# Batch 0 in two token ranges, ordered first loads, and a table of convolution blocks and priorities per batch, in a pooled-attention and gated-FFN kernel

## The chip, the cores and the metric

One core of a Trainium2 chip. The metric is the time of one execution on the device, in microseconds (us), median of several runs. The span in a profile is the time from the first to the last instruction of the profiled run and is about 2 us shorter. Engines are called PE (matmul), DVE (vector), ACT (scalar), POOL (GpSimd) and SP (which issues the stores and a few loads), as the profile does. The granted clock is the share of PE's full clock that the profile records.

## The reference, cut to what matters

```python
# q, k, v: (8 batches, 8 heads, 576 tokens, 64)
k_p = k.reshape(B, H, 72, 8, D).mean(axis=3)          # pool 8 tokens into one
v_p = v.reshape(B, H, 72, 8, D).mean(axis=3)
attn = softmax(q @ k_p^T / sqrt(D)) @ v_p             # -> x: (8, 576, 512)
h = np.maximum(x @ w_in, 0.0)                         # w_in: 512 x 1024
conv_out = sum_k conv_w[k] * hp[:, k:k + S, :]        # 3 taps along the tokens, per channel
gate = 1.0 / (1.0 + np.exp(-conv_out))
out = (h * gate) @ w_out                              # w_out: 1024 x 512
```

Inputs and output are fp32. The kernel computes in bf16, and takes the sigmoid as (1 + tanh)/2, so that one set of activation functions serves exp and tanh.

## The kernel before

The program is built by a small planner. Each piece of work is an `Op` with an assumed duration on each engine that may do it, its dependences, and a priority. The planner walks forward in assumed time, gives each engine the ready piece with the lowest priority number, and writes the instructions out in that order. Each engine's list is then fixed. A piece that may run on DVE or ACT is placed when the plan is made, not on the chip.

```python
class Planner:
    N_PS = 4            # PSUM slots, each 2 x 512 fp32
    WARM = 24.0         # fill PE's idle time with matmuls on zeros up to here
    ...
        for e, c in per.items():
            t0 = min(c)[0]
            c = [x for x in c if x[0] <= t0 + 0.02]
            s, p, i = min(c, key=lambda x: (x[1], x[2]))      # p is the priority
```

The 1024 hidden channels are eight blocks of 128. The three-tap convolution of a block exists in two forms. On PE it is three matmuls with diagonal weights for each half of the tokens. Off PE it is three scalings on DVE or ACT, two additions on DVE, and a tanh on ACT:

```python
    def conv_off(b, f, pr):
        ...
        for kk in (1, 0, 2):
            pl.add(f"cp{kk}.{b}.{f}", {"DVE": 0.225, "ACT": 0.59}, ...)   # cv = factor * shifted hT
        for kk in (0, 2):
            pl.add(f"ca{kk}.{b}.{f}", "DVE", 0.375, ...)                  # cv[1] += cv[kk]
        pl.add(f"tanh.{b}.{f}", "ACT", 0.59, ...)
    def conv_pe(b, f, pr):
        ...
        for kk in range(3):
            for i in range(2):
                nc.tensor.matmul(out=t[:, i, 0:HC], lhsT=dw[:, f, kk, :], rhs=hT[m][:, f, ...], ...)
        pl.add(f"conv.{b}.{f}", "PE", 0.745, ...)
    def conv(b, f, pr):
        conv_off(b, f, pr) if f in OFF[b] else conv_pe(b, f, pr)
        # then on DVE for every block: tg = tg + 1, and gT = tg * hT   (the gate product)
```

`OFF` is (1, 3, 5, 7) for every batch. Priorities follow one rule for all batches: `mm1` (the product with `w_in`) of block f at 8b + f, its convolution 1.3 later, the next batch's attention at fixed offsets, `mm2` (the product with `w_out`) of a pair of batches at 11.0, 14.5, 10.5, 12.5 and 15.5. Batch 0's k is loaded as fp32 on SP's queue, q and v as bf16 on POOL's queue.

The softmax here doesn't subtract the row's maximum and nothing guards it: scores larger than these inputs give would overflow.

Of the kernel before, what the change touches and what calls it, by code (L numbers as in the profile page):

```python
# [14 lines left out]

class Op:
# [3 lines left out]
class Planner:  # L20
# [7 lines left out]
    WARM = 24.0  # L28
# [37 lines left out]
    def order(self):  # L66
# [10 lines left out]
        live = set()  # L77
# [4 lines left out]
        while avail:  # L82
            best = None
            per = {}
            for i, t in avail.items():
                o = ops[i]
                st = t
                if o.take is not None and o.take not in held:
                    if not slots:
                        continue  # L90
                    st = max(st, min(slots.values()))
                cand = None
                for e, d in o.eng.items():
                    s = max(st, free.get(e, 0.0))
                    if cand is None or s + d < cand[0]:
                        cand = (s + d, s, e)
                _, s, e = cand
                per.setdefault(e, []).append((s, o.prio, i))
# [14 lines left out]
            if e == "PE" and s < self.WARM and s - free.get(e, 0.0) > 0.3:  # L113
                f0 = max(free.get(e, 0.0), 0.6)
                x = min(slots, key=lambda y: (slots[y], y)) if slots else None
                if x is not None and slots[x] <= f0 and s - f0 > 0.3:
                    self.gaps[i] = (s - f0, x)
# [7 lines left out]
            if o.give is not None:  # L125
                slots[held[o.give]] = o.done
            out.append((s, e, d, o))
# [12 lines left out]
def kernel(  # L140
# [40 lines left out]
    k_f = st("k_f", [KR, KT, 512], FP32)  # L181
# [21 lines left out]
    OFF = [(1, 3, 5, 7) for b in range(B)]  # L203
# [13 lines left out]
    def warm(gap, x):  # L217
        t = pp.tile([P, 2, 512], FP32, name="psw", tag=f"ps{x}")
        for _ in range(min(int((gap - 0.2) / 0.1), 60)):
            nc.tensor.matmul(out=t[:, 0, 0:P], lhsT=zero[:, 0:P], rhs=zero[:, 0:P], start=True, stop=True)  # L220
# [30 lines left out]
    def load_k(b, prio):  # L251
        m = b % 2
        if b == 0:
            for i in range(2):
                def fn(e, i=i):
                    nc.sync.dma_start(out=k_f[:, 3 * i:3 * i + 3, :], in_=rows_k(0)[:, 3 * i:3 * i + 3, :])
                pl.add(f"ldk0.{i}", "SP", 0.6, fn, writes=[("kf", i)], prio=prio, nbytes=H * S * D * 2)
        else:
            def fn(e):
                nc.gpsimd.dma_start(out=k_b[m], in_=rows_k(b))  # L260
            pl.add(f"ldk{b}", "POOL", 0.9, fn, writes=[("k", m)], prio=prio, nbytes=H * S * D * 4)

    def load_v(b, prio):
        m = b % 2

        def fn(e):
            nc.gpsimd.dma_start(out=v_b[m], in_=rows_v(b))
        pl.add(f"ldv{b}", "POOL", 0.9, fn, writes=[("v", m)], prio=prio, nbytes=H * S * D * 4)
# [15 lines left out]
    def consts():  # L284
# [6 lines left out]
        pl.add("ident", "POOL", 0.6, fn, writes=["ident"], prio=-50)  # L291
# [17 lines left out]
        def fn(e):  # L309
            t = slot("cw")  # L310
            nc.tensor.transpose(out=t[:, 0, 0:24], in_=cw_raw, identity=identf)
        pl.add("cwT", "PE", 0.1, fn, reads=["cwr", "identf"], writes=["cwp"], prio=-46, take="cw")

        def fn(e):
            nc.vector.tensor_scalar(out=cw, in0=slot("cw")[:, 0, 0:24], scalar1=2.0, scalar2=None, op0=OP.mult)
        pl.add("cw", "DVE", 0.1, fn, reads=["cwp"], writes=["cw"], prio=-45, give="cw")

        for f in range(n_fb):
            for kk in range(3):
                def fn(e, f=f, kk=kk):  # L320
                    s = cw[:, kk * n_fb + f:kk * n_fb + f + 1]
                    if e == "ACT":
                        nc.scalar.activation(out=dw[:, f, kk, :], in_=ident, func=ACT.Copy, scale=s)
                    else:
                        nc.vector.tensor_scalar(out=dw[:, f, kk, :], in0=ident, scalar1=s, scalar2=None, op0=OP.mult)
                pl.add(f"dw{f}.{kk}", {"ACT": 0.3, "DVE": 0.2}, 0, fn, reads=["cw", "ident"],
                       writes=[("dw", f, kk)], prio=-3 + 0.5 * f)
# [13 lines left out]
    def attn_k(b, pr):  # L341
        m = b % 2
        if b == 0:
            for i in range(2):
                def fn(e, i=i):
                    c = slice(3 * i, 3 * i + 3)
                    nc.vector.tensor_tensor(out=kp1[:, c, :], in0=k_f[:, c, 0:256], in1=k_f[:, c, 256:512], op=OP.add)
                pl.add(f"kp1.{b}.{i}", "DVE", 0.875, fn, reads=[("kf", i)], writes=[("kp1", i)], prio=pr)
# [34 lines left out]
    def attn_v(b, pr):  # L383
        m = b % 2

        def fn(e):
            nc.vector.tensor_tensor(out=vp1, in0=v_b[m][:, :, 0:256], in1=v_b[m][:, :, 256:512], op=OP.add)
        pl.add(f"vp1.{b}", "DVE", 1.14, fn, reads=[("v", m)], writes=["vp1"], prio=pr)

        def fn(e):  # L390
            nc.vector.tensor_tensor(out=vp2, in0=vp1[:, :, 0:128], in1=vp1[:, :, 128:256], op=OP.add)
        pl.add(f"vp2.{b}", "DVE", 0.61, fn, reads=["vp1"], writes=["vp2"], prio=pr)
# [3 lines left out]
        pl.add(f"va.{b}", "DVE", 0.34, fn, reads=["vp2", ("v8", m)], writes=[("va", m)], prio=pr)  # L396
# [20 lines left out]
    def attn_s(b, h, pr):  # L417
        m = b % 2
        key = ("sc", b, h)

        def fn(e):
            t = slot(key)
            for par in range(2):
                nc.tensor.matmul(  # L424
                    out=t[0:Sp, par, 0:HC],
                    lhsT=kTz[m][:, par, h * Sp:(h + 1) * Sp],
                    rhs=qT[m][:, :, h * A:(h + 1) * A],
                    start=True, stop=True,
                )
        pl.add(f"sc.{b}.{h}", "PE", 0.25, fn,  # L430
               reads=[("kTz", m, 0), ("kTz", m, 1), ("qT", m, 0), ("qT", m, 1), ("qT", m, 2)],
               writes=[("scp", b, h)], prio=pr, take=key)

        def fn(e):
            nc.scalar.activation(  # L435
                out=attnT[m][:, h, :].rearrange("p (c i x) -> p i c x", i=2, x=32),
                in_=slot(key)[0:Sp, :, 0:HC].rearrange("p i (c x) -> p i c x", x=32),
                func=ACT.Exp, scale=1.0 / 64.0,
            )
        pl.add(f"exp.{b}.{h}", "ACT", 0.55, fn, reads=[("scp", b, h)], writes=[("at", m, h)], prio=pr, give=key)  # L440

    def attn_av(b, t, pr):
# [11 lines left out]
        pl.add(f"av.{b}.{t}", "PE", 0.36, fn, reads=[("at", m, h) for h in range(H)] + [("va", m)],  # L454
# [36 lines left out]

    def mm1(b, f, pr):
        m = b % 2
# [14 lines left out]
        pl.add(f"relu.{b}.{f}", "ACT", 0.55, fn, reads=[("hp", b, f)], writes=[("hT", m, f)], prio=pr, give=key)  # L508
# [3 lines left out]
    def conv_off(b, f, pr):  # L512
# [4 lines left out]
        for kk in (1, 0, 2):  # L517
# [7 lines left out]
            pl.add(f"cp{kk}.{b}.{f}", {"DVE": 0.225, "ACT": 0.59}, 0, fn, reads=[("hT", m, f), ("hz", m), "cw"],  # L525
# [10 lines left out]
    def conv(b, f, pr):  # L536
# [14 lines left out]
        pl.add(f"g.{b}.{f}", "DVE", 0.375, fn, reads=[("tg", i3), ("hT", m, f)], writes=[("gT", (b // 2) % 2, f, b % 2)],  # L551
               prio=pr)

    def conv_pe(b, f, pr):
# [11 lines left out]
        pl.add(f"conv.{b}.{f}", "PE", 0.745, fn, reads=[("hT", m, f), ("hz", m)] + [("dw", f, kk) for kk in range(3)],  # L566
# [9 lines left out]
    def mm2(pair, tiles, pr):  # L576
# [4 lines left out]
        for x, t in enumerate(tiles):  # L581
            halves = [0] if t < 4 else ([0, 1] if t == 4 else [1])

            def fn(e, x=x, t=t):
                a = slot(key)
                for c in range(n_fb):
                    nc.tensor.matmul(out=a[:, x, :], lhsT=g[:, c, t * P:(t + 1) * P], rhs=w_out[:, c, :],  # L587
                                     start=(c == 0), stop=(c == n_fb - 1))
            pl.add(f"mm2.{pair}.{t}", "PE", 1.74, fn,
                   reads=[("gT", pair % 2, c, y) for c in range(n_fb) for y in halves] + [("wo", 0), ("wo", 1)],  # L590
                   writes=[("op", pair, t)], prio=pr, take=key)
# [12 lines left out]
    def loads(b, prio):  # L604
        load_k(b, prio)
        load_q(b, 1 if b else 3, prio + 0.01)
        load_v(b, prio + 0.02)

    def attn(b):
        o = 8.0 * (b - 1)  # L610
        attn_k(b, o - 2.0)
        attn_q(b, [o - 1.5, o - 1.3, o - 1.1])
        attn_v(b, o + 0.0)
        for h in range(H):
            attn_s(b, h, o + 0.55 * h)
        for t in range(n_t):
            attn_av(b, t, o + 5.0 + 0.4 * t)
# [4 lines left out]
    loads(1, -20)  # L622
    weights_out(-25)
    attn(0)
    for b in range(B):
# [5 lines left out]
        for f in range(n_fb):  # L631
            mm1(b, f, o + f)
            conv(b, f, o + f + 1.3)
        p = b // 2
        if b % 2 == 0:
            mm2(p, (0, 1), o + 11.0)
            mm2(p, (2, 3), o + 14.5)
        else:
            mm2(p, (4,), o + 10.5)
            mm2(p, (5, 6), o + 12.5)  # L640
            mm2(p, (7, 8), o + 15.5)
# [37 lines left out]
```

## Time and profile before

The time is 246.21 us (244.66 to 247.72, 3 runs); the profiled span is 243.0 us.

| stage | what sets the pace | number |
|---|---|---|
| start, to the first `xT,w_in` matmul | loads, then one chain through DVE, ACT, PE | 25.42 us |
| middle | PE | 97% of 82 to 182 us |
| end, after the last gate product | `mm2` of four tiles, copy, store | 12.3 us (243.0 - 230.7) |

The page of the kernel before: busy time of each engine with its share of the span, then two rows of forty equal slices (tenths of busy PE, tenths of granted PE clock), then the chain of work that ended last.

```profile
PE 217.2 (89%) x1877; PEld 153.1 (63%) x1877; DVE 174.1 (72%) x470; ACT 165.5 (68%) x269; POOL 26.5 (11%) x47
...
PE   8566996589979999899999999999999999999691
...
PEclk9996799959999999999999999999999999999999
...
PE 56%; DVE 19%; ACT 19%; DMA 3%; issue 1%; ACTq 0%; DVEq 0%; POOLq 0%
```

PE leads the chain. Its weak slices stand in the first quarter and at the end. The timeline of the kernel before shows the start (columns: start, duration, engine, line, operation, output<-input, and in brackets the idle time before it):

```profile
8.50 0.51 PE L407 MATMUL psb<-ident,q_b 128*128 128x128 bf16 x6 [2.30 <-DMA q_b<-in_q_dram]
...
9.52 0.94 DVE L347 TENSOR_TENSOR kp<-k_f 96x768 bf16<-96x768 f32 x1
...
14.70 4.41 ACT L435 ACTIVATE attnT<-psf 72x576 bf16<-72x576 f32 x8
...
25.42 1.84 PE L500 MATMUL psf<-xT,w_in 128*128 128x288 bf16 x7
```

The second half of k is pooled only at 9.52 us, the exps over all tokens start at 14.70, and then all five token tiles of the attention output must pass before `xT,w_in` starts.

Busy time by stretch, kernel before (columns: from:to and length in us; busy us and instruction count of PE, weight loads, DVE, ACT, POOL; granted clock; DMA share; GB/s):

```profile
36.00:42.00 6.00, 4.26 (x45) 3.27 (x44) 5.92 (x15) 5.48 (x10) 0.58 (x1) 1.00 1.27 194
42.00:48.00 6.00, 3.38 (x45) 2.23 (x45) 5.86 (x15) 4.27 (x8) 1.56 (x2) 0.97 1.15 202
48.00:54.00 6.00, 4.80 (x48) 4.17 (x46) 5.03 (x14) 2.61 (x4) 0.36 (x1) 0.50 1.04 146
...
82.00:134.00 52.00, 50.64 (x452) 35.88 (x450) 44.00 (x115) 40.55 (x67) 2.63 (x3) 1.00 0.48 104
134.00:182.00 48.00, 46.51 (x414) 32.44 (x413) 32.92 (x96) 36.02 (x59) 0.00 (x0) 1.00 0.15 48
```

From 36 to 48 us DVE is full and PE is not; after that the clock is halved for six microseconds. From 82 us on PE is full and DVE has room: 76.9 busy of 100 us.

The end, in the chain of the kernel before (start, duration, what):

```profile
230.25 0.47 DVE gT L550
230.72 0.05 issue
230.77 7.31 PE psf L587 x33
...
238.15 1.01 ACT osb L595
```

### The profile page before, as it was taken

Reading aid. Unit: us, or ns where it says so; the run is one execution under the profiler, and the core shown is the slowest. Engines: PE = TensorE matmul, PEld = TensorE weight load, DVE = VectorE, ACT = ScalarE, POOL = GpSimd, SP = SyncE. Lnnn points to the kernel's source line nnn. Section 1 sums busy time; section 2 is a strip of 40 time slices with the busy share of each in tenths; the row PEclk is TensorE's granted clock in tenths of the full one; section 3 lists DMA queues with packets and bytes.
Section 4 is the critical chain, followed back from the end, with each engine's and each line's share of the span. In section 5 each row is a group of like instructions: output and inputs, shape, how many; then the busy total and the mean of one; then the engine's idle time right before and its main releaser. Section 6 shows DMA issues by size and latency. Waiting matters only on the chain.

```text
span 243.0 us, 4692 instructions
## 1 busy us (share of the span) xinstructions
PE 217.2 (89%) x1877; PEld 153.1 (63%) x1877; DVE 174.1 (72%) x470; ACT 165.5 (68%) x269; POOL 26.5 (11%) x47
## 2 busy tenths in 40 slices
PE   8566996589979999899999999999999999999691
PEld 8444775467656766666768667676767767656340
DVE  2597399989699997995499657933987659447500
ACT  2192399649795996769857967687949957657421
POOL 7843010212111220000000000000000000000000
PEclk9996799959999999999999999999999999999999
DMA  7999999999994998052204412020202101102214
GB/s 171 203 199 208 207 210 194 199 126 147 172 191 96 182 184 186 29 101 86 86 3 108 79 46 86 3 86 3 86 0 89 43 26 63 72 21 83 86 62 153
DMA packets 20617, 26.59 MB, mean 109 GB/s; under 512 B 2396, under 2 KB 14516, under 8 KB 20596
## 3 DMA queue, kind: packets, MB, share of 16 engines
q0 software_dynamic: 15024, 15.67, 40.4%
q1 hardware_dynamic: 5572, 10.63, 12.6%
q8 instruction: 14, 0.23, 0.4%
q14 instruction: 7, 0.06, 0.1%
HBM read 32.52 MB, written 9.44 MB: 173 GB/s over the span
## 4 chain that ended last, share of the span: by engine, by line
PE 56%; DVE 19%; ACT 19%; DMA 3%; issue 1%; ACTq 0%; DVEq 0%; POOLq 0%
PE psf L587 25%; PE psf L500 17%; ACT hT L506 5%; PE psf L563 4%; ACT attnT L435 4%; PE psf L424 4%; DVE xx L465 3%; DMA q_b<-in_q_dram 3%; PE psb L479 3%; ACT osb L595 3%; DVE cv L524 2%; DVE cv L529 2%; PE psb L407 2%; ACT cv L522 2%; ACT tg L533 2%; ACT tg L570 2%
## 5 line engine op out<-in xcount | busy, mean ns | idle before, releaser
L500 PE MATMUL psf<-xT,w_in 128*128 128x288 bf16 x512 | 72.3, 288 | 0.7
L587 PE MATMUL psf<-w_out,gT 128*128 128x512 bf16 x288 | 65.9, 379 | 2.4 <-DVE gT L550 1.9
L500 PEld LDWEIGHTS <-w_in 128*128 128x128 bf16 x512 | 50.0, 98 | 15.4 <-issue 2.0
L506 ACT ACTIVATE hT<-psf 128x576 bf16<-128x576 f32 x64 | 41.5, 651 | 13.4 <-PE psf L500 13.2
L587 PEld LDWEIGHTS <-gT 128*128 128x128 bf16 x288 | 27.7, 98 | 32.5 <-DVE gT L550 2.6
L524 DVE TENSOR_SCALAR cv<-hT,cw 128x576 bf16<-128x576 bf16 x76 | 24.2, 367 | 28.4 <-ACT hT L506 28.2
L435 ACT ACTIVATE attnT<-psf 72x576 bf16<-72x576 f32 x64 | 39.9, 652 | 0.6 <-PE psf L424 0.5
L595 ACT COPY osb<-psf 128x1024 f32<-128x1024 f32 (+1 forms) x20 | 18.5, 927 | 25.2 <-PE psf L587 25.2
L533 ACT ACTIVATE tg<-cv 128x576 bf16<-128x576 bf16 x32 | 21.8, 687 | 11.8 <-DVE cv L529 11.7
L550 DVE TENSOR_TENSOR gT<-tg,hT 128x576 bf16<-128x576 bf16 x64 | 29.1, 455 | 0.8
L563 PE MATMUL psf<-hT,dw 128*128 128x288 bf16 x192 | 29.0, 286 | 0.0
L529 DVE TENSOR_TENSOR cv<-cv 128x576 bf16<-128x576 bf16 x64 | 28.5, 445 | 0.4
L424 PE MATMUL psf<-qT,kTz 128*72 128x288 bf16 x128 | 24.8, 287 | 3.6 <-DVE qT L413 1.9
L545 DVE TENSOR_SCALAR tg<-tg 128x576 bf16<-128x576 bf16 x64 | 19.5, 304 | 11.7 <-ACT tg L533 11.7
L465 DVE TENSOR_TENSOR xx<-psf,rr 128x512 bf16<-128x512 f32 x40 | 27.1, 684 | 0.2
L479 PE MATMUL psb<-perm,xx 128*128 128x128 bf16 x160 | 17.6, 240 | 5.3 <-DVE xx L465 4.7
L570 ACT ACTIVATE tg<-psf 128x576 bf16<-128x576 f32 x32 | 20.7, 646 | 0.8
L563 PEld LDWEIGHTS <-dw 128*128 128x128 bf16 x192 | 18.2, 97 | 4.5
L424 PEld LDWEIGHTS <-kTz 128*72 128x72 bf16 x128 | 14.4, 114 | 8.3 <-issue 4.7
L452 PE MATMUL psf<-vaug,attnT 72*128 72x65 bf16 x320 | 16.3, 196 | 2.8 <-ACT attnT L435 1.3
L479 PEld LDWEIGHTS <-xx 128*128 128x128 bf16 x160 | 11.9, 106 | 10.3 <-DVE xx L465 8.0
L452 PEld LDWEIGHTS <-attnT 72*128 72x128 bf16 x320 | 14.3, 100 | 5.4 <-ACT attnT L435 3.3
(46 smaller groups left out, 181.0 us busy)
## 6 DMA issues: line engine op xcount, KB each, us to landing
out_dram<-osb SPq DMA_DIRECT2D x16, 512.0 KB, 2.8
v_b<-in_v_dram POOLq DMA_DIRECT2D x8, 576.0 KB, 11.0
k_b<-in_k_dram POOLq DMA_DIRECT2D x7, 576.0 KB, 11.4
q_b<-in_q_dram POOLq DMA_DIRECT2D x7, 576.0 KB, 10.3
k_f<-in_k_dram SPq DMA_DIRECT2D x2, 576.0 KB, 5.8
w_in<-in_moe_w_in_dram POOLq DMA_DIRECT2D x4, 256.0 KB, 10.9
w_out<-in_moe_w_out_dram POOLq DMA_DIRECT2D x2, 512.0 KB, 14.6
out_dram<-osb SPq DMA_DIRECT2D x4, 256.0 KB, 2.0
```

Source lines behind the costliest of these rows:

```text
L424: nc.tensor.matmul(out=t[0:Sp, par, 0:HC], lhsT=kTz[m][:, par, h * Sp:(h + 1) * Sp], rhs=qT[m][:, :, h * A:(h + 1) * A], start=True, stop= ...
L435: nc.scalar.activation(out=attnT[m][:, h, :].rearrange("p (c i x) -> p i c x", i=2, x=32), in_=slot(key)[0:Sp, :, 0:HC].rearrange("p i (c ...
L452: nc.tensor.matmul(out=a[:, h // 4, c:c + D + 1], lhsT=attnT[m][:, h, u0:u0 + 128], rhs=vaug[m][:, h, :], start=True, stop=True)
L465: nc.vector.tensor_tensor(out=xx[i3].rearrange("p (g h e) -> p g h e", g=2, h=4), in0=av_view()[:, :, :, 0:D], in1=rr[i3].rearrange("p (g ...
L479: nc.tensor.transpose(out=a[:, 0, c * P:(c + 1) * P], in_=xx[i3][:, c * P:(c + 1) * P], identity=perm)
L500: nc.tensor.matmul(out=t[:, i, 0:HC], lhsT=w_in[:, c, f * P:(f + 1) * P], rhs=xT[m][:, c, i * HC:(i + 1) * HC], start=(c == 0), stop=(c == ...
L506: nc.scalar.activation(out=hT[m][:, f, 2:S + 2].rearrange("p (i x) -> p i x", i=2), in_=slot(key)[:, :, 0:HC], func=ACT.Relu, scale=0.5)
L524: nc.vector.tensor_scalar(out=cv[y][:, kk, :], in0=src, scalar1=s, scalar2=None, op0=OP.mult)
L529: nc.vector.tensor_tensor(out=cv[y][:, 1, :], in0=cv[y][:, 1, :], in1=cv[y][:, kk, :], op=OP.add)
L550: nc.vector.tensor_tensor(out=gT[(b // 2) % 2][:, f, o:o + S], in0=tg[i3], in1=hT[m][:, f, 2:S + 2], op=OP.mult)
L563: nc.tensor.matmul(out=t[:, i, 0:HC], lhsT=dw[:, f, kk, :], rhs=hT[m][:, f, 1 + kk + i * HC:1 + kk + (i + 1) * HC], start=(kk == 0), stop= ...
L587: nc.tensor.matmul(out=a[:, x, :], lhsT=g[:, c, t * P:(t + 1) * P], rhs=w_out[:, c, :], start=(c == 0), stop=(c == n_fb - 1))
```

## The change

The intent: start `mm1` of batch 0 when two thirds of its tokens are ready; load in the order of need on one queue; take more convolution blocks off PE, by a table for each batch, and set every group of priorities by a table, so that PE, DVE and ACT are filled together; shorten the end. The diff, cut to its core:

```diff
+PARAMS = {
+    "off": [(2, 3, 4, 7), (1, 3, 4, 5, 6), (0, 1, 2, 3, 5, 7), (0, 1, 2, 3, 4, 6, 7), (1, 2, 3, 4, 5, 6, 7), (0, 1, 2,
+        3, 4, 5, 6, 7), (0, 1, 2, 3, 4, 5, 6, 7), (0, 1, 2, 3, 4, 5, 6)],
+    "k": [-6.89, -4.22, ...], "q": [...], "v": [...], "s": [...], "ds": [...], "av": [...],
+    "conv": [4.85, 4.34, 4.9, 2.85, 2.38, 2.01, 3.44, 4.85],
+    "mm2": [6.99, 13.56, 11.95, 11.64, 14.87, ...],
+}
-    WARM = 24.0
+    WARM = 60.0
+    QUOTA = {"sc": 2, "o": 2}                  # at most two PSUM slots for scores, two for mm2
-    OFF = [(1, 3, 5, 7) for b in range(B)]
+    OFF = PARAMS["off"]
...
-                    nc.sync.dma_start(out=k_f[:, 3 * i:3 * i + 3, :], in_=rows_k(0)[...])
+                    nc.gpsimd.dma_start(out=k_b[0][:, 3 * i:3 * i + 3, :], in_=rows_k(0)[...])
...                                             # v of batch 0 in two halves; diagonal weights on POOL
+        parts = [(0, 6, (0, 1)), (6, 9, (2,))] if b == 0 else [(0, 9, (0, 1, 2))]     # scores and exps
...
+    def mm1_parts(b, f, pr):                   # batch 0: mm1 and relu in two token ranges
+        for x, (j0, j1, ts) in enumerate([(0, 24, (0, 1, 2)), (24, 36, (3, 4))]):
...
-            mm2(p, (4,), o + 10.5)
-            mm2(p, (5, 6), o + 12.5)
-            mm2(p, (7, 8), o + 15.5)
+            mm2(p, (4,), o + m2[2], 6 if last else n_fb)       # last pair: 6 of 8 channel blocks first
+            mm2(p, (5, 6), o + m2[3], 6 if last else n_fb)
+            for g in ((7,), (8,)) if last else ((7, 8),):
+                mm2(p, g, o + m2[4])
```

The table holds 52 blocks instead of 32, so 12 blocks stay on PE instead of 32.

## The prediction

"Unbroken" in this and the later texts is the time of an instruction from its start to the start of the next, when the next follows at once: an addition of a constant on DVE lasts 0.30 us by itself, and 0.22 us unbroken. Sums of such times are the work of an engine without waits.

> **What bounds the kernel now.** Page: PE 217.2 us busy of 243.0 (89%), DVE 174.1, ACT 165.5; chain 56% PE, 19% DVE, 19% ACT. Three stages:
>
> 1. Start. The first first-layer matmul (`xT,w_in`) runs at 25.42 us (timeline). Until then the chain is: DMA of `q_b` to 8.45, DVE on k to 11.64, eight exps on ACT 14.70 to 19.12 (waiting for all of q and k), then five attention tiles in a row.
> 2. Steady state. The chain's pattern recurs every 51.9 us per two batches, 26.0 per batch, with PE 96 to 99% busy per 20 us stretch (stages table), DVE 60 to 91%. PE-bound. Batches 0 and 1 are worse: between 36 and 54 us PE is idle 5.6 of 18 us behind DVE (98% busy from 36 to 48), and the granted clock falls to 0.50 at 48 to 54.
> 3. Tail. The last gate product ends at 230.72, then 33 second-layer matmuls take 7.31 us, the copy 1.01, the store about 3; PE waited some 3 us before.
>
> **What the change moves**.
> PE: convolution 192 to 72 matmuls; six take 0.74 us, so 20 blocks save 14.8. PE's unbroken work is about 201 us before (fillers excluded), 186 after.
> DVE: 40 more adds (0.37), 27 more scalings (0.22), some copies; 19 identity scalings leave for POOL. Unbroken about 163 before, 185 after; busy 174 to about 200.
> ACT: scalings 20 to 53 (0.67), some copies to DVE: 165 to about 183 busy.
> So DVE becomes a co-limit. The Trainium skill, "VectorE: DVE Perf Modes" (section on why `tensor_tensor` can't do 4×), caps adds at half the scalings' best rate; the trace agrees: 0.37 against 0.22 us for 576 columns.
>
> Start: k first at about 330 GB/s of fp32 source (estimate: bytes landed by 15 us), whole near 7 us, q near 10.5, v near 14; exps from about 10.5; three tiles, not five, gate the first matmul: about 20 us instead of 25.4.
> Tail: only 22 matmuls (4.8 us) follow the last gate product, the last store is half as large, and 18 matmuls fill PE's wait: 3 to 6 us less.
> Middle: per batch PE needs on average 23.3 us, DVE 23.0 unbroken. With both nearly full I expect waits: 24.5 per batch instead of 26.0.
>
> **Sum.** PE: 20 before the first matmul, 181 of remaining work, 3.8 after: 205. DVE: 20 + 176 + 9: 205 too. Before, the same PE sum is 226 against 243: 17 lost to waits and clock. After, I give 13: span 218, time about 221 us. Start's 5.5 and the tail's gain are all critical; of the conv's 14.8 about 10 should survive.
>
> **What would show it.** First `xT,w_in` matmul at 19 to 21.5 us; PE and DVE each near 200 busy, ACT 183; DVE's share of the chain 30% or more; 48 to 50 us per two batches; no half clock between 48 and 60 us (the Trainium skill, "TensorE: Matmul & The Clock Gate", Part 1: idle stretches halve the clock; the trace agrees at 0.50); under 9 us after the last gate product.
>
> **What would make it wrong.** The plan fixes each engine's order from assumed durations; where the chip differs (ACT scaling 0.67 against 0.59 assumed), two nearly full in-order engines stall each other, and only start and tail remain (about 235). Ordered loads could come late. The 21 POOL scalings may be slow and delay loads behind them. Tuned priorities could hide more: 212.

## The result, and the profile after

The changed kernel takes 220.31 us median (218.99 to 220.89, 4 runs), against 245.44 for the kernel before in the runs beside it. The ratio is 0.8957 (95% interval 0.8878 to 0.9036). Ratios here and below are the mean time of one kernel's fast runs over that of the other's in the same rounds, so they are not quite the ratio of the medians quoted. Executions over 1.5% slower than the fastest of the same kernel are left out of the means.

The page of the changed kernel, the same rows as above, with DVE's slices added:

```profile
PE 201.8 (93%) x1800; PEld 140.8 (65%) x1816; DVE 191.4 (88%) x531; ACT 175.0 (81%) x303; POOL 34.9 (16%) x71
...
PE   8987998799999999889989999999999999999992
...
DVE  0668299999999999999999999999999999999910
...
PEclk9996799999999999999999999999999999999998
...
DVE 58%; PE 21%; ACT 13%; DMA 3%; issue 2%; POOL 1%; another core or an unknown queue 1%; ACTq 0%; DVEq 0%; POOLq 0%
```

The chain has changed hands: DVE 58%, PE 21%. A reduced clock remains in the fourth and fifth slices, while the one near 50 us is gone. The start in the timeline of the changed kernel:

```profile
6.81 0.56 DVE L368 TENSOR_TENSOR kp<-k_b 96x768 bf16<-96x768 bf16 x1
...
9.35 0.51 PE L433 MATMUL psb<-ident,q_b 128*128 128x128 bf16 x6
...
12.08 4.87 ACT L464 ACTIVATE attnT<-psf 72x384 bf16<-72x384 f32 x16 [0.61 <-PE psf L453]
...
20.68 1.44 PE L531 MATMUL psf<-xT,w_in 128*128 128x384 bf16 x4 [0.52 <-DVE xT L515]
```

k is pooled 2.7 us earlier, q comes 0.85 us later (it now stands behind k on the one queue), and the first `xT,w_in` matmul runs at 20.68 instead of 25.42 us. But its first four matmuls take 1.44 us. The stretches of the changed kernel show why, and show the middle:

```profile
18.00:24.00 6.00, 5.06 (x36) 3.32 (x35) 3.92 (x9) 1.22 (x3) 5.94 (x19) 0.51 1.20 210
...
82.00:134.00 52.00, 49.03 (x459) 35.09 (x463) 51.36 (x138) 45.79 (x78) 3.49 (x5) 1.00 0.51 109
134.00:182.00 48.00, 46.70 (x425) 32.43 (x427) 47.75 (x145) 46.96 (x77) 0.00 (x0) 1.00 0.14 50
```

The clock is at 0.51 from 18 to 24 us, just where the first `mm1` runs. In the 100 us of the middle DVE is busy 99.1, PE 95.7 and ACT 92.8: three engines nearly full at once. The end, in the timeline of the changed kernel:

```profile
204.37 8.85 PE L642 MATMUL psf<-w_out,gT 128*128 128x512 bf16 x39
...
206.54 0.83 DVE L604 TENSOR_TENSOR gT<-tg,hT 128x576 bf16<-128x576 bf16 x2
...
207.43 5.51 PEld L642 LDWEIGHTS <-gT 128*128 128x128 bf16 x27 [0.27 <-DVE gT L604]
...
213.51 0.59 ACT L652 COPY osb<-psf 128x512 f32<-128x512 f32 x1 [1.18 <-remote]
```

After the last gate product (207.4) 9.8 us are left, 2.5 less than before. From the first `xT,w_in` to the end of the last `mm2` it is 192.5 us (20.7 to 213.2) instead of 212.7 (25.4 to 238.1), so 24.1 us a batch instead of 26.6. The shortening is not even. The 64 gate products (eight for each batch) can be counted in the two traces, as the `gT<-tg,hT` instructions of DVE in order of time: of the 25.8 us by which the span falls, 8.4 are gained by the end of the 16th (84.9 to 76.5 us), 5.8 from there to the 48th (102.9 to 97.1), 9.1 in the last sixteen (42.9 to 33.8), and 2.5 after the last.

### The profile page after: what moved, and what is told of

It is laid out like the page before. It is cut to its first block, busy times and chain, and to the rows that moved or that the text cites. A ratio compares the mean times of both kernels' runs of the same rounds, so it can differ in the third digit from the quotient of the medians.

```text
span 217.2 us, 4675 instructions
## 1 busy us (share of the span) xinstructions
PE 201.8 (93%) x1800; PEld 140.8 (65%) x1816; DVE 191.4 (88%) x531; ACT 175.0 (81%) x303; POOL 34.9 (16%) x71
## 4 chain that ended last, share of the span: by engine, by line
DVE 58%; PE 21%; ACT 13%; DMA 3%; issue 2%; POOL 1%; another core or an unknown queue 1%; ACTq 0%; DVEq 0%; POOLq 0%
DVE cv L583 12%; DVE cv L578 10%; PE psf L642 9%; DVE xx L495 8%; DVE gT L604 7%; PE psf L554 6%; ACT attnT L464 5%; DVE tg L599 5%; DMA q_b<-in_q_dram 3%; DVE vp L411 3%; DVE qT L439 2%; ACT cv L576 2%; DVE kp L372 2%; DVE kTz L400 2%; PE psf L531 2%
## 5 line engine op out<-in xcount | busy, mean ns | idle before, releaser
L554 PE MATMUL psf<-xT,w_in 128*128 128x288 bf16 x448 | 62.1, 286 | 1.2 <-DVE xT L515 0.5
L554 PEld LDWEIGHTS <-w_in 128*128 128x128 bf16 x448 | 42.9, 98 | 13.1 <-DVE xT L515 1.0
L583 DVE TENSOR_TENSOR cv<-cv 128x576 bf16<-128x576 bf16 x104 | 46.0, 449 | 0.4 <-DVE cv L578 0.2
L464 ACT ACTIVATE attnT<-psf 72x576 bf16<-72x576 f32 (+2 forms) x72 | 39.3, 613 | 1.1 <-PE psf L453 1.1
L576 ACT ACTIVATE cv<-hT,cw 128x576 bf16<-128x576 bf16 x53 | 39.2, 772 | 0.4 <-DVE cv L583 0.2
L587 ACT ACTIVATE tg<-cv 128x576 bf16<-128x576 bf16 x52 | 35.7, 695 | 3.0 <-DVE cv L583 2.4
L578 DVE TENSOR_SCALAR cv<-hT,cw 128x576 bf16<-128x576 bf16 x103 | 34.9, 363 | 2.6 <-ACT hT L538 2.5
L453 PE MATMUL psf<-qT,kTz 128*72 128x288 bf16 (+2 forms) x144 | 24.3, 271 | 2.2 <-DVE qT L439 0.6
L509 PEld LDWEIGHTS <-xx 128*128 128x128 bf16 x160 | 11.2, 102 | 9.2 <-DVE xx L495 5.8
L515 DVE COPY xT<-psb 128x512 bf16<-128x512 bf16 (+1 forms) x29 | 11.0, 390 | 2.4 <-PE psb L509 2.3
L287 POOL DMA_DIRECT2D v_b<-in_v_dram x9 | 7.5, 834 | 27.7 <-DVE vp L411 14.1
```

The source lines that it names most:

```text
L453: nc.tensor.matmul(out=t[0:Sp, par, 0:n], lhsT=kTz[m][:, par, h * Sp:(h + 1) * Sp], rhs=qT[m][:, 2 * c0:2 * c1, h * A:(h + 1) * A], start= ...
L464: nc.scalar.activation(out=attnT[m][:, h, :].rearrange("p (c i x) -> p i c x", i=2, x=32)[:, :, c0:c1, :], in_=slot(key)[0:Sp, :, 0:n].rea ...
L554: nc.tensor.matmul(out=t[:, i, 0:HC], lhsT=w_in[:, c, f * P:(f + 1) * P], rhs=xT[m][:, c, i * HC:(i + 1) * HC], start=(c == 0), stop=(c == ...
L576: nc.scalar.activation(out=cv[y][:, kk, :], in_=src, func=ACT.Copy, scale=s)
L578: nc.vector.tensor_scalar(out=cv[y][:, kk, :], in0=src, scalar1=s, scalar2=None, op0=OP.mult)
L583: nc.vector.tensor_tensor(out=cv[y][:, 1, :], in0=cv[y][:, 1, :], in1=cv[y][:, kk, :], op=OP.add)
```

## The experiments

My theory, T: the middle was bound by PE, the change takes 14.8 us off PE and fills DVE instead, and the priorities are needed to keep both full. Rival R1: the priorities alone do it. Rival R2: the table alone does it. Times are medians; "before" beside these runs was 245.64 to 246.54 us. The 95% intervals of the ratios reach 0.003 to 0.009 to each side.

| run | time, us | ratio to before |
|---|---|---|
| changed kernel | 220.31 | 0.8957 |
| a_off4: four blocks a batch again | 234.28 | 0.9504 |
| a_oldprio: old priorities again (3 fast runs of 4) | 234.74 | 0.9520 |
| a_base: both undone | 237.58 | 0.9665 |
| b_off: before, with the table alone | 241.28 | 0.9786 |
| a_dve, a_pe: changed, more DVE / PE work | 232.58, 227.83 | 0.9414, 0.9259 |
| b_dve, b_pe: before, more DVE / PE work | 250.18, 260.39 | 1.0183, 1.0587 |
| a_late: first loads later | 222.35 | 0.9059 |
| a_heat: batch 0's scores twice | 217.14 | 0.8844 |
| r_plan: a_heat, refitted | 215.83 | 0.8749 |
| r_pool: r_plan's way, one step to POOL | 251.26 | 1.0170 |

### Table and priorities, alone and together

```diff
 # a_off4                                        # a_oldprio
-    OFF = PARAMS["off"]                         -    "conv": [4.85, 4.34, 4.9, ...]
+    OFF = [(1, 3, 5, 7) for b in range(B)]      +    "conv": [1.3] * 8    (and all others as before)
 # a_base: both.   # b_off: the kernel before with the table of 52 blocks.
```

> The changed kernel with one part undone: four conv blocks a batch off TensorE (1, 3, 5, 7) as before, all else (start, priorities, quota, tail) kept. My theory (the middle is worth 1.5 to 2.5 us a batch and comes from taking 20 blocks off PE): PE gets 14.8 us back, so 228 to 234 us, DVE's share of the chain falls well below 58% and PE's rises above 40%. Rival R1 (the priorities and the pipelining they give do it, the table matters little): within 2% of the changed kernel, at most 224 us.

> The changed kernel with the old priorities (one rule for all batches), table, start, quota and tail kept. My theory: the orders no longer fit two nearly full engines, DVE falls from 98% busy in the middle to about 90%, so 226 to 234 us. R2 (table and start do it): at most 223 us. R1: the whole middle gain is lost, over 236 us.

> The kernel before with the table of conv blocks alone (52 blocks off PE instead of 32), old priorities, old start, old tail. My theory: the middle becomes DVE-bound but the old priorities leave waits, so about a third to a half of the gain: 232 to 241 us, first xT,w_in matmul still near 25.4 us. Rival R2 (the table is the change, priorities immaterial): 229 to 232 us, that is all but the start and the tail.

> The changed kernel with both the table and the priorities undone: start, quota, fillers and tail are left. The three corners measured are 220.3 (both), 234.3 (priorities alone) and 235.4 (table alone). If start and tail are worth the 7 to 9 us that the two timelines show at both ends (first xT,w_in 4.7 us earlier, end 2.5 us nearer to the last gate product): 236 to 240 us, and then table and priorities are worth little alone (1 to 5 us each) and about 17 together. If the parts simply add: 249 us, which would leave nothing for start and tail.

Three of the four came out at or just past the slow end of what T expected (234.3 for up to 234, 234.7 for up to 234, 241.3 for up to 241); a_base fell inside, at 237.6. In a_off4 the chain went back to PE as expected (PE 66%, DVE 20%). In a_oldprio DVE was busy for 95% of the middle, not for about 90%. The four corners that share the new start and end, as ratios to before:

| | old priorities | new priorities |
|---|---|---|
| 32 blocks off PE | 0.9665 | 0.9504 |
| 52 blocks off PE | 0.9520 | 0.8957 |

Start, end, quota and fillers together give 3.4% (8 us). On top of that the table alone gives 1.5% (3.6 us) and the priorities alone 1.6% (4 us), but together they give 7.1% (17 us). Neither R1 nor R2 stands: more than half of this gain, 4.0% (give or take 1.4, from the four intervals), exists only with both. The stretches show how full the engines were. This is a_off4, then a_oldprio, then a_base, all from 82 to 134 and 134 to 182 us:

```profile
82.00:134.00 52.00, 51.54 (x456) 36.14 (x454) 48.29 (x124) 40.55 (x68) 2.66 (x4) 1.00 0.49 103
134.00:182.00 48.00, 47.27 (x440) 34.22 (x439) 35.91 (x101) 36.83 (x60) 0.00 (x0) 1.00 0.14 51
```

```profile
82.00:134.00 52.00, 47.89 (x420) 33.23 (x419) 50.73 (x140) 43.89 (x72) 2.66 (x4) 1.00 0.52 110
134.00:182.00 48.00, 44.68 (x400) 30.84 (x399) 44.26 (x131) 42.70 (x71) 0.00 (x0) 1.00 0.14 51
```

```profile
82.00:134.00 52.00, 50.51 (x451) 35.77 (x450) 43.87 (x116) 40.51 (x67) 2.75 (x4) 1.00 0.46 101
134.00:182.00 48.00, 46.65 (x427) 33.37 (x425) 33.47 (x95) 35.44 (x58) 0.00 (x0) 1.00 0.14 50
```

With 32 blocks off, PE is at 97.2 of 100 us under the old priorities (a_base), and the new ones can only bring it to 98.8 (a_off4): its work was the limit. With 52 blocks off under the old priorities (a_oldprio) neither is full, PE 92.6 and DVE 95.0: much of the work taken off PE turned into waits between engines whose orders are fixed. With the new priorities both are fuller (DVE 99.1, PE 95.7 in the changed kernel).

These stretches don't hold most of the surplus, though. Here is the count of gate products in the four traces (end of the 16th, 48th and 64th, and the span, in us). The last column sums the time at half clock, times one half.

| | 16th | 48th | 64th | span | lost clock |
|---|---|---|---|---|---|
| a_base | 79.8 | 182.0 | 224.9 | 233.8 | 1.7 |
| a_off4 | 82.6 | 181.3 | 221.4 | 231.5 | 5.9 |
| a_oldprio | 80.0 | 181.5 | 219.0 | 231.5 | 6.9 |
| changed | 76.5 | 173.6 | 207.4 | 217.2 | 4.0 |

From the 16th to the 48th product the table alone gains 0.7 us, the priorities alone 3.5, both 5.1; from the 48th to the 64th it is 5.4, 2.8 and 9.1. In both stretches the parts nearly add. Of the surplus of 12.0 us in these four runs, 6.3 arise before the 16th product and 3.9 after the last. Just there the half clock differs too: each change alone lost over 4 us more of clock than a_base. If every such microsecond counted in full, the half clock would make about 7 of the 12 us (an estimate from the last column). So that both changes are needed together is shown; how much of their surplus is plain waiting and how much the half clock is not, since no run kept the clock whole in all four corners.

One more limit of this test is that the priorities came with the table, and others made for 32 blocks could beat a_off4; that was not tried.

### Which engine binds, before and after

```diff
 # a_dve, b_dve: one more addition of a constant for each of the 64 blocks, its result unused
             nc.vector.tensor_scalar(out=tg[i3], in0=tg[i3], scalar1=1.0, ..., op0=OP.add)
+            nc.vector.tensor_scalar(out=junk, in0=hT[m][:, f, 2:S + 2], scalar1=1.0, ..., op0=OP.add)
 # a_pe, b_pe: the first channel chunk of each mm1 twice (the second starts the sum anew: same result)
+            for i in range(2):
+                nc.tensor.matmul(out=t[:, i, 0:HC], lhsT=w_in[:, 0, f * P:(f + 1) * P], rhs=..., start=True, stop=True)
```

The planner is not told, so the orders stay. (The expectations call the added DVE piece a scaling; what was built is an addition of 1, which takes 0.22 us unbroken in the trace.) The DVE runs add 64 x 0.22 = 14.1 us of work, the PE runs 64 x 0.245 = 15.7 us.

> The changed kernel with 64 more scalings on DVE (one per block, 0.22 us unbroken, 14 us in all), their result unused, order otherwise the same, the planner not told. If DVE binds the middle, as its 58% of the chain says: 10 to 14 us slower (slope 0.7 to 1). If PE and DVE share the limit through waits: 5 to 9 us. If PE binds: under 4 us.

> The changed kernel with the first pass of each first-layer product done twice (576 columns more per block, 0.245 us, 15.7 us of PE work in all, same result), the planner not told. If DVE binds the middle: PE's idle 4 to 7% there takes some of it, 5 to 10 us slower (slope 0.3 to 0.65). If PE binds: 13 us or more.

> The kernel before with the same 64 scalings more on DVE (14 us of DVE work). PE-bound as predicted: DVE has 20 to 40% room in the middle, so 2 to 5 us slower, all of it in the first two batches and where a chain passes through DVE. If DVE already bound it: 10 us or more.

> The kernel before with the same 15.7 us of PE work more. PE-bound as predicted: 12 to 16 us slower (slope 0.8 to 1). If not PE-bound: under 8 us.

| | more DVE work | of it shows | more PE work | of it shows |
|---|---|---|---|---|
| before | + 4.2 us | 30% | + 14.4 us | 92% |
| changed | + 12.3 us | 87% | + 7.5 us | 48% |

(Differences of medians over the work added; from the ratios the four are 4.5, 14.4, 11.2 and 7.4 us.) All four fall where T put them. Before, PE binds and DVE has room. After, DVE leads, and PE is close behind: half of what is put on it shows. By the ratios and their intervals the two shares of the changed kernel are 80% (59 to 101) for DVE and 47% (32 to 62) for PE, so the order of the two is likely and not certain. The chain of a_dve and then of a_pe, from their pages:

```profile
DVE 74%; PE 11%; ACT 7%; DMA 3%; issue 2%; POOL 1%; DVEq 0%; ACTq 0%; POOLq 0%
```

```profile
PE 74%; DVE 16%; ACT 8%; issue 1%; ACTq 0%
```

15.7 us more of PE work are enough to hand the chain back to PE. The changed kernel stands near the balance.

### Does the start reach the end?

```diff
 # a_late
+                    if i == 0:
+                        nc.gpsimd.dma_start(out=k_j, in_=rows_k(7))      # k_j is not used
                     nc.gpsimd.dma_start(out=k_b[0][:, 3 * i:3 * i + 3, :], ...)
```

> The changed kernel with one load of 1.18 MB of source, its result unused, put ahead of k on the same queue: all first loads come about 3.6 us later (estimate from some 330 GB/s), orders unchanged. If the start is all on the critical path, as predicted: 3 to 4.5 us slower, first xT,w_in matmul at 24 to 25 us. If DVE's backlog in the middle absorbs it: under 1.5 us.

The first `xT,w_in` matmul moved by 2.8 us, to 23.49 (timeline of a_late), less than the 3.6 estimated. The time rose by 2.0 us in medians, 2.5 by the ratios. So most of a shift at the start reaches the end, and neither reading in the expectation was quite right. In the two profiled runs nothing is absorbed: a_late is 2.8 us behind at the first `xT,w_in` matmul, 4.0 at the eighth gate product (55.8 for 51.8 us), after one more half-clock stretch of 3.4 us from 45.3 us on, and 3.9 at the end. The medians lie closer because the other three runs of the changed kernel had a lower mean clock than its profiled one (0.965 to 0.977 for 0.982), and those of a_late did not (0.977 to 0.985 for 0.977).

```profile
23.49 1.44 PE L534 MATMUL psf<-xT,w_in 128*128 128x384 bf16 x4 [0.52 <-DVE xT L518]
```

### The half clock under the first mm1

```diff
 # a_heat
-                for par in range(2):
+                for par in (0, 1, 0, 1) if b == 0 else (0, 1):
                     nc.tensor.matmul(out=t[0:Sp, par, 0:n], lhsT=kTz[m][...], rhs=qT[m][...], start=True, stop=True)
```

> The changed kernel with every score matmul of batch 0 done twice (same result), in PE's slack behind the exps from 12 to 16 us. The granted clock there fell to 0.51 at 18 to 24 us, and the first xT,w_in matmuls took 1.44 us for four. If PE's idle share before causes it and the loss is critical: clock 0.9 or more at 18 to 24 us, four matmuls in about 0.7 us, 1 to 2.5 us faster in all. If DVE sets the pace from there on: clock restored, time within 0.7 us. If idle time at 16 to 18 us causes it: clock and time unchanged.

The two stretches around the loss in the changed kernel (the first line) and in a_heat (the other two), and a_heat's first `xT,w_in` matmuls in the timeline:

```profile
12.00:18.00 6.00, 4.93 (x66) 3.62 (x64) 4.14 (x11) 4.87 (x16) 3.62 (x10) 1.00 1.40 197
```

```profile
12.00:18.00 6.00, 5.65 (x96) 5.21 (x93) 4.02 (x11) 4.84 (x16) 3.58 (x10) 1.00 1.40 197
18.00:24.00 6.00, 5.04 (x55) 3.68 (x53) 3.93 (x10) 2.84 (x7) 5.94 (x18) 1.00 1.20 211
```

```profile
20.14 0.81 PE L531 MATMUL psf<-xT,w_in 128*128 128x384 bf16 x4 [0.52 <-DVE xT L515]
```

The clock is whole at 18 to 24 us, and four matmuls take 0.81 us instead of 1.44. The time is 217.14 us, 3.2 less in medians and 2.8 by the ratios: somewhat more than expected, and its six runs lie closer together (216.70 to 217.57) than the changed kernel's four. Between the two profiled runs it is 1.9 us, nearly all of it gained by the eighth gate product (51.8 to 50.0 us); the rest goes with the changed kernel's other runs, whose mean clock was lower still, while a_heat's was 0.997 or more in all six. The Trainium skill, "TensorE: Matmul & The Clock Gate", Part 1, says that the clock is halved by idle windows of about 3.4 us. Here no idle gap that long exists: between 12 and 18.7 us the longest that the timeline lists before a PE instruction is 0.43 us. But between 12.5 and 16.4 us PE only fed exps, in short bursts. The same page, section "A second HAM failure mode: psum-queue depth-cycling", says that frequent micro-idles between groups of matmuls can halve the clock too; the changed kernel and a_heat agree with that. (In the kernel before, too, no idle gap of PE listed in the 6 us ahead of the half clock at 47.6 us is over 0.96 us.) Doing the score matmuls twice, in PE's slack and with no new wait, kept the clock in all six runs of a_heat.

It is no sure remedy. r_plan, the next run, does them twice as well, and its profiled run lost the clock from 20.9 us on for 3.4 us, although PE was busier before than in a_heat:

```profile
12.00:18.00 6.00, 5.76 (x96) 5.41 (x94) 3.56 (x8) 4.86 (x16) 3.22 (x9) 1.00 1.40 196
18.00:24.00 6.00, 4.78 (x45) 2.95 (x42) 4.51 (x12) 1.08 (x2) 5.89 (x17) 0.74 1.21 211
```

Its first four `xT,w_in` matmuls took 1.44 us again. Of r_plan's six runs, two had a mean clock of 0.991 and 0.992 and took 217.03 and 217.40 us; the other four, at 0.998 and above, took 214.91 to 215.98. So the busy share at 12 to 18 us alone doesn't decide, and the same kernel can keep or lose the clock from run to run.

### A refit, and a step moved to POOL

The planner assumes 0.225 us on DVE and 0.59 on ACT for a convolution scaling; the chain shows 0.28 (three in 0.84) and 0.67 (two in 1.33). For ACT the Trainium skill, "ScalarE: Activation LUTs", section "What ACT_TABLE_LOAD costs", gives about 93 ns for each per-partition operand; the trace agrees: 0.67 us for the scaling, with such a factor, against 0.58 for a tanh of the same 576 columns with a constant one. Both durations were corrected in the planner, and table and priorities were searched again by random steps against the planner's own span. In r_pool, besides, the "+ 1" of batches 1 to 6 was given to POOL, with six tanh buffers instead of three.

```diff
 # r_plan, on top of a_heat (new PARAMS, 48 blocks)
-            pl.add(f"cp{kk}.{b}.{f}", {"DVE": 0.225, "ACT": 0.59}, ...)
+            pl.add(f"cp{kk}.{b}.{f}", {"DVE": 0.285, "ACT": 0.67}, ...)
 # r_pool, on top of that (own PARAMS, 55 blocks)
-        pl.add(f"tg1.{b}.{f}", "DVE", 0.225, ...)
+        pl.add(f"tg1.{b}.{f}", {"POOL": 0.8} if 0 < b < B - 1 else {"DVE": 0.225}, 0, ...)
```

> a_heat (the changed kernel with batch 0's score matmuls done twice, 217.1 us) with a new table and new priorities, found by random steps against the planner's own assumed span after two of its assumed durations were set to what the traces show (scaling by a per-partition factor: DVE 0.225 to 0.285, ACT 0.59 to 0.67 us). 48 blocks off TensorE instead of 52. If wrong assumed durations cost stalls in the changed kernel: 211 to 215 us. If the given table was already as good as the chip allows (fitted by other means): 216 to 219 us.

> The same as r_plan, and the 48 additions of 1 to the tanh of batches 1 to 6 moved from DVE to POOL (six tanh buffers instead of three), table and priorities fitted for that. It takes 10.6 us of unbroken work off DVE, the engine of which 14 us more cost 12.3. If DVE's load is what binds and POOL does one in about 0.8 us (estimate from 0.35 for 128 columns and 0.57 for a 576-column memset): 208 to 213 us, DVE busy under 185. If POOL takes over 1.2 us each or slows DVE at the memory: no gain over r_plan or a loss.

r_plan takes 215.83 us (ratio 0.8749, interval 0.8719 to 0.8780; a_heat's was 0.8813 to 0.8874, in another round). It is the fastest kernel, but it fell between the two ranges, and table, priorities and durations changed together. That the wrong durations had cost something is likely, at about 1%, and not isolated.

r_pool failed: 251.26 us, 1.7% slower than the kernel before (1.3 to 2.1). One POOL and one DVE group of r_pool, then the same DVE line in the changed kernel (count, then busy us and mean ns of one, then idle time before):

```profile
L597 POOL TENSOR_SCALAR tg<-tg 128x576 bf16<-128x576 bf16 x48 | 92.2, 1926 | 61.9 <-ACT tg L585 51.5
...
L576 DVE TENSOR_SCALAR cv<-hT,cw 128x576 bf16<-128x576 bf16 x117 | 50.5, 457 | 1.4 <-ACT hT L536 1.3
```

```profile
L578 DVE TENSOR_SCALAR cv<-hT,cw 128x576 bf16<-128x576 bf16 x103 | 34.9, 363 | 2.6 <-ACT hT L538 2.5
```

One "+ 1" takes 1.93 us on POOL on average, at least 1.64 (the profile's spans on POOL are rough), where 0.8 was assumed and DVE takes 0.30. The diagonal weights in the changed kernel had shown it: 0.36 us for 128 columns is 2.8 ns a column, and 576 columns at that rate are 1.6 us. The estimate of 0.8 had mixed that with a memset, which is another operation. Besides, DVE's own scalings rose from 363 to 457 ns on average (the median stayed at 362, the longest went from 489 to 939), so single ones were held up. The Trainium skill, "GPSIMD Engine Reference", section "Key points", says that POOL shares its SBUF interfaces with DVE and that certain DVE instructions contend for them; r_pool's own trace agrees with it. The DVE scalings with no POOL addition beside them lasted 366 ns on average (63 of them), those wholly beside one 586 (27); for the gate products it was 446 (44) and 692 (15). The DVE products that read PSUM (`xx`) stayed at 679 (25) and 683 (13). That breaks the premise: DVE was busy 210.7 us, not under 185. How much of the loss is this, and how much the slow additions on POOL, the runs don't separate.

## Why the prediction was right

The predicted time was 221 us and the measured one 220.3; the span 218 and 217.2. Point by point:

- **What bound the kernel before: right.** 92% of added PE work shows, 30% of added DVE work.
- **DVE becomes a co-limit: right, and it probably leads.** Its chain share is 58% (30% or more was predicted), and 87% of added DVE work shows. PE is near: 48%.
- **Start: right in size, with two parts wrong.** The first `xT,w_in` matmul was put at 20 us and runs at 20.68. k (whole near 7) and v (near 14) came as said. The exps start at 12.08, not 10.5: they need two thirds of q, and PE takes the second third up at 10.37. The way from there to the first matmul took 8.6 us, where the prediction's figures give 9.5, and so more than half of this delay was made up. And the half clock, promised away for 48 to 60 us and indeed gone there (1.00), stands at 18 to 24 us, where I did not look for it: 2 us (the profiled runs) to 3 us (the medians and ratios), by a_heat.
- **Tail: too good.** 9.8 us remain after the last gate product, not under 9, since 27 weight loads and not 22 follow it. That is 2.5 us less than before, where 3 to 6 were predicted. Start, tail, quota and fillers give 8 us together (a_base); 8.5 to 11.5 was the sum predicted.
- **Middle: right in size, wrong as a split.** From the 16th to the 48th gate product a batch takes 24.3 us instead of 25.7, and 24.5 instead of 26.0 was predicted. But the saving was not spread over all batches like that: 9.1 of the 25.8 us come in the last two, where the table leaves one block of sixteen on PE, and the prediction doesn't single them out. And "of the conv's 14.8 about 10 should survive" treats the table as a term of its own. Alone it is worth 3.6 us and the priorities 4; together they are worth 17. The last term of the sum depends on two changes at once.
- **The total: partly luck.** The 13 us of waits and lost clock that the sum left were given, not worked out. Start and tail then gained less than said and the rest more, and the errors balanced to within 1 us.
- **Sizes.** Busy times came out lower than said: DVE 191.4 for "about 200", ACT 175.0 for 183. Where an engine is full, its instructions overlap (one "+ 1" on DVE lasts 0.30 us, two in a row 0.53), so the busy measure moves towards the unbroken sum (185 for DVE). A scaling was taken as 0.22 us on DVE; that is the "+ 1" with a constant, and the scaling by a per-partition factor takes 0.28. For 27 more that is 1.6 us.
- **What could have made it wrong.** Two full engines stalling each other is what a_oldprio shows, at 234.7 us, close to the figure given for that case; the lost clock has a part in it. The given priorities avoid most of it.

## What to carry to other kernels

When one engine is full and the others have room, moving work off it may pay little until the order of work is refitted for the new balance: here table and priorities were worth 3.6 and 4 us alone and 17 together, so test such changes as a pair and not one at a time. Look at the granted clock of every run that is compared, since a new order can lose or keep it. To learn which engine binds, add a known amount of unused work to one engine without changing the order, and see how much of it shows in the time. Before moving an operation to another engine, scale a duration of the same operation there by its size, not one of a similar operation.

## What the Trainium skill lacked or had wrong

- "TensorE: Matmul & The Clock Gate" ties the half clock to idle windows of about 3.4 us in Part 1, and mentions micro-idles in the section on its second failure mode, but gives no busy share at which they halve it. In the changed kernel PE was 4.93 of 6 us busy at 12 to 18 us by the profile's measure, no idle gap listed there or up to 18.7 us was over 0.43 us, and yet the clock fell to 0.51 at 18 to 24 us; with the score matmuls done twice (5.65 of 6 us) it stayed at 1.00, and the time went from 220.3 to 217.1 us. A busy share alone may not be the rule: in r_plan it was 5.76 of 6 us, and the clock at 18 to 24 us was 0.74.
- "GPSIMD Engine Reference", section "Engine selection", calls one-input elementwise operations roughly line rate on POOL. Here a one-input addition of a constant on 576 bf16 columns took 1.64 us at the least (1.93 on average), and a scaling of 128 columns 0.36 us: 2.8 ns a column. DVE takes 0.30 us for the 576.
- "VectorE: DVE Perf Modes", section "Scalar operands", gives no cost for a per-partition factor. Unbroken, a 576-column bf16 scaling with such a factor took 0.28 us, and an addition of a constant 0.22. The shift of two of the three scalings' sources by a token is not the cause: the third reads the unshifted tile, and three in a row still take 0.84 us, while the addition put into a_dve reads that same tile at 0.22 us. The operand or the multiplication in place of an addition is left; no run separates these.
